# Linear attention's denominators through DRAM, and key-value products of 65 columns

## The chip, the cores and the metric

The kernel runs on one core of one Trainium2 chip. The metric is the device time of one execution in microseconds (us). Times of the kernel before: 1421.81 us, the median of 3 runs (1420.85 to 1428.24).

## What is computed

Three layers follow each other: a linear attention, a feed-forward layer with an ELU, and a mixture of four experts. The change lies in the first.

```python
def phi(x):                                    # 4 batches, 8 heads, 576 tokens, 64 wide; w_phi 64 x 128
    proj = einsum('bhsd,df->bhsf', x, w_phi)
    proj = proj - max(abs(proj), axis=-1)
    return concatenate([exp(proj), exp(-proj)])
q_p, k_p = phi(q), phi(k)
kv  = einsum('bhsf,bhsd->bhfd', k_p, v)
z   = sum(k_p, axis=2)
num = einsum('bhsf,bhfd->bhsd', q_p, kv)
den = einsum('bhsf,bhf->bhs', q_p, z) + 1e-06
x   = num / den                                # 2304 tokens x 512
h   = x @ w_in;  x = where(h > 0, h, exp(min(h, 0)) - 1) @ w_out
x   = sum over 4 experts of p_e * (relu(x @ w1[e]) @ w2[e])
```

## The kernel before

The attention goes over 16 pairs of heads (4 batches, 4 pairs each); `pair(i)` is a Python generator that emits the instructions of one pair in 11 pieces, with a `yield` between pieces. The pieces: project keys and queries with `wbd` (L199 and L221 for pairs 0 to 6 in plain fp32, L201 to L203 as three products of fp32r halves from pair 7 on), subtract the row's largest absolute value (`guard`, L209 and L210 on DVE), take both exponentials on ACT, form the key-value products (`kv`, L242 and L243, 20 matmul instructions a pair with 128x128 weights from `kp` or `kpm` and 128 moving columns from `vt`), transpose the queries' features (L249, L287), and multiply them with the key-value products (`num`, L321, in two halves of 288 tokens).

The tile `vt` holds, for each block of keys, 64 columns of values and 64 columns of ones (L165 fills the tile with 1.0 once, `load` writes the values over one half). So the rows of a `num` result are 64 numerators and 64 equal copies of the denominator. `num` copies the denominators out of PSUM on ACT (L325), `divide` takes the reciprocal of 128x288 on DVE (L330) and multiplies the numerators, still in PSUM, by it (L333). `put_x` stores the result `xf` in DRAM (L301, for a later pass) and splits it into `xh` and `xl` (L307 on ACT, L308 on POOL), which the second stage reads.

The second stage (`Elu`, L530 to L532 up, L559 to L561 down) goes over 9 tiles of 256 tokens, twice (two halves of the hidden width). Tile t of the first half needs all pairs of its batches: 4 pairs before tile 0, 8 before tile 2, 12 before tile 4, 16 before tile 6. Between its instructions `slot()` emits further pieces of the attention (1.4 to a slot) and of the weight conversions. Where a tile's pairs are not yet emitted, L758 emits pieces until they are. `convert64` turns a block of weights into two fp32r halves: a load on SP (L104) into one of three buffers, then ACT, DVE (L115 to L118), POOL, ACT and POOL in turn; 64 such loads belong to the first half. The third stage (`Up`, `Down`) is untouched by the change.

All DMAs are issued on the one SP queue, in order: an issue that waits holds all behind it. A scheduler puts the emitted instructions of each engine into one fixed order when the program is built. The pair's tiles `kq`, `xf` and `rc` have one buffer each, the PSUM pool `bank` has seven.

Of the kernel before, what the change touches and what calls it, by code (L numbers as in the profile page):

```python
# [8 lines left out]
F32 = mybir.dt.float32  # L9
F32R = mybir.dt.float32r  # L10
U32 = mybir.dt.uint32
I64 = mybir.dt.int64
ACTF = mybir.ActivationFunctionType
ALU = mybir.AluOpType
# [3 lines left out]
B, H, S, D, FEAT = 4, 8, 576, 64, 128  # L18
NT, DM, DFF, E, F2 = 2304, 512, 2048, 4, 1024
P = 128  # L20
KD = DM // P
NP = H // 2
# [32 lines left out]
CVP = 16  # L55
CVW = 256
CVOFF = 0
MINF = 2.0 ** -15
MAXF = 122879.9921875

# [2 lines left out]
def attn_elu_moe_kernel(ctx: ExitStack, tc: tile.TileContext, kq_in, vv, w_phi, w_in, w_out, probs, w1, w2, out):  # L63
# [13 lines left out]
    x1fin = [dram.tile([P, KD, TS], F32, name=f"x1fin{t}") for t in range(NTS)]  # L77
    yscr = [dram.tile([P, DM], F32, name=f"yscr{r}") for r in range(NT // P)]
    xvd = [[dram.tile([P, 2, 2, TC], F32, name=f"xvd{g}_{k}") for k in range(7)] for g in range(NG)]
    x1scr = [dram.tile([P, KD, TS], F32, name=f"x1scr{t}") for t in range(NTS)]  # L80
    ring = pool("ring", RING)
    p2 = ExitStack()
# [55 lines left out]
    def load(i):  # L138
        b, p = divmod(i, NP)
        kq = ld.tile([P, 2 * S], F32, tag="kq", name="kq")  # L140
        SP.dma_start(kq[:, :640], kq_in[b, p, :, :640])
        if i == 0:
            SP.dma_start(wbd, w_phi)
        SP.dma_start(kq[:, 640:], kq_in[b, p, :, 640:])
        v = vt[i % 2]
        SP.dma_start(v[:, 0:4, 0:D], vv[b, p, :, 0:4, :])
        SP.dma_start(v[:, 4:8, D:P], vv[b, p, :, 4:8, :])
        SP.dma_start(v[0:D, 8, 0:D], vv[b, p, 0:D, 8, :])
        SP.dma_start(v[0:D, 9, D:P], vv[b, p, D:P, 8, :])
        return kq, v  # L150

    def bank(shape=(P, 512)):
        return psum[0].tile(list(shape), F32, tag="bank", name="bank")
# [7 lines left out]

    make_identity(nc, ident)
    for i in range(2):
        t = a1.tile([P, 10, P], F32, name=f"vt{i}")
        G.memset(t, 1.0)  # L165
        vt.append(t)
    kpm = a1.tile([P, 2, 2, P], F32, name="kpm")
# [8 lines left out]
    def pair(i):  # L176
# [58 lines left out]
        yield  # L235
        guard(qd[1], proj(qh, 1), 4)
        yield
        pk = bank((P, 4, P))

        def kv(h, c):  # L240
            for t in range(4):
# [30 lines left out]
                G.tensor_tensor(out=el[:, h, :, c0:c0 + n], in0=ef[:, h], in1=f32(eh[:, h, :, c0:c0 + n]), op=ALU.subtract)  # L272

        if wide:
            kvw = a1.tile([P, 4, P], F32, tag=("kvh", "kvl")[i % 2], name="kvw")
        else:
            kvh = a1.tile([P, 4, P], F32R, tag="kvh", name="kvh")
            kvl = a1.tile([P, 4, P], F32R, tag="kvl", name="kvl")
        ef0 = qexp(tpose(0), 0, 256)
        kv(0, 0)  # L280
        kv(0, 1)
# [26 lines left out]
                G.tensor_tensor(out=xl[:, p, c:c + n], in0=xf[:, o:o + n], in1=f32(xh[:, p, c:c + n]), op=ALU.subtract)  # L308
                o += n

        rc = a1.tile([P, 2, HS], F32, tag="rc", name="rc")

        def num(s):
            sl = slice(s * HS, (s + 1) * HS)
            pn = [bank() for _ in range(2)]
            terms = ((kvw, ew),) if wide else ((kvh, eh), (kvh, el), (kvl, eh))
            last = 2 * len(terms) - 1
            for h in range(2):
                for k in range(last + 1):
                    c, (w, m) = k // len(terms), terms[k % len(terms)]  # L320
                    PE.matmul(pn[h][:, :HS], w[:, 2 * h + c], m[:, h, c, sl], start=(k == 0), stop=(k == last))  # L321
            for h in range(2):
                r = slice(h * D, h * D + D)
                o = slice(D - h * D, P - h * D)
                A.activation(rc[r, s], pn[h][o, :HS], ACTF.Copy, bias=1e-6)  # L325
            return pn

        def divide(s, pn):
            sl = slice(s * HS, (s + 1) * HS)
            V.reciprocal(out=rc[:, s], in_=rc[:, s])  # L330
            for h in range(2):
                r = slice(h * D, h * D + D)
                V.tensor_tensor(out=xf[r, sl], in0=pn[h][r, :HS], in1=rc[r, s], op=ALU.mult)  # L333

        pn0 = num(0)
        yield
        divide(0, pn0)
        pn1 = num(1)
        yield
        divide(1, pn1)  # L340
        put_x()

    done = [0]
# [545 lines left out]
```

## Time and profile before

| | |
|---|---|
| median of 3 runs | 1421.81 us |
| the profiled execution | 1429.35 us, its span 1427.6 us |
| PE busy | 1385.5 us, 97% |
| PE weight loads busy | 1292.6 us, 91% |
| DVE, ACT, POOL busy | 687.9, 618.2, 440.8 us |
| mean granted TensorE clock | 0.991 of full speed |
| DMA | 160.22 MB, 112 GB/s |

The trace shows two matmuls, each with its weight load, for one plain fp32 matmul instruction of the program (L199, L221, L242, L243, and L321 of pairs 0 to 6), and one for a transpose or an fp32r matmul; so the 20 key-value instructions of a pair stand there as 40.

Busy time of PE is a union of matmul durations that overlap each other, so a busy PE can still issue slowly; what counts is the spacing from one matmul's start to the next. The attention and the first half of the second stage lie in the first 450 us, the third stage in the last 770.

### The profile page before, as it was taken

The numbers are of one execution on the slowest core, as the hardware profiler recorded it, in microseconds if no ns is written. First come the engines' busy times: TensorE is split into PE (matmuls) and PEld (weight loads), VectorE is DVE, ScalarE is ACT, GpSimd is POOL, SyncE is SP. The second block draws the span as 40 slices with busy tenths as digits, with TensorE's granted clock in tenths as the row PEclk, the third lists the DMA queues.
The fourth block names the chain that finished last, engine by engine and source line by source line (L and its number), as shares of the span: only waits on it lengthen the run. The fifth ranks groups of instructions, "written<-read, shape, count | busy, mean of one in ns | idle before, by whom it ended". The sixth has DMA issues, their size and how long they took to land.

```text
span 1427.6 us, 22324 instructions
## 1 busy us (share of the span) xinstructions
PE 1385.5 (97%) x8688; PEld 1292.6 (91%) x8688; DVE 687.9 (48%) x1150; ACT 618.2 (43%) x1348; POOL 440.8 (31%) x499
## 2 busy tenths in 40 slices
PE   7899999999999999999999999999999999999998
PEld 6788999999999999999998989898888989899897
DVE  7987756565477635334434323234433325323332
ACT  6766866666466534344333443122321214321121
POOL 4556754444377713024102340002320005300000
PEclk9999999999999999999999999999999999999999
DMA  5324322120333345313333233434145351433421
GB/s 156 125 87 132 111 62 60 56 70 32 97 98 126 97 159 198 112 46 104 111 133 147 93 107 137 155 111 148 47 146 177 101 200 54 141 111 133 165 79 67
DMA packets 93625, 160.22 MB, mean 112 GB/s; under 512 B 28496, under 2 KB 39888, under 8 KB 93520
## 3 DMA queue, kind: packets, MB, share of 16 engines
q1 hardware_dynamic: 93520, 158.80, 33.6%
q8 instruction: 68, 1.11, 0.3%
q14 instruction: 37, 0.30, 0.1%
HBM read 109.22 MB, written 49.55 MB: 111 GB/s over the span
## 4 chain that ended last, share of the span: by engine, by line
PE 75%; DMA 5%; DVE 4%; ACT 2%; POOL 2%; issue 2%; SPq 0%; DVEq 0%; ACTq 0%; POOLq 0%
PE bank L706 8%; PE bank L707 8%; PE bank L708 8%; PE bank L647 7%; PE bank L649 7%; PE bank L648 7%; PE bank L560 3%; PE bank L559 3%; PE bank L561 3%; PE bank L530 3%; PE bank L532 3%; PE bank L531 3%; PE bank L242 2%; DMA wst<-in_w 2%; PE bank L321 2%
## 5 line engine op out<-in xcount | busy, mean ns | idle before, releaser
L706 PE MATMUL bank<-w,h 128*128 128x512 f32 x576 | 224.6, 392 | 4.7 <-ACT h L658 4.7
L648 PE MATMUL bank<-xv,w 128*128 128x384 f32 x672 | 226.1, 336 | 0.0
L707 PE MATMUL bank<-w,h 128*128 128x512 f32 x576 | 225.6, 392 | 0.0
L647 PE MATMUL bank<-xv,w 128*128 128x384 f32 x672 | 223.8, 339 | 1.0 <-DVE xs L580 0.8
L649 PE MATMUL bank<-xv,w 128*128 128x384 f32 x672 | 223.0, 337 | 0.0
L708 PE MATMUL bank<-w,h 128*128 128x512 f32 x576 | 198.3, 391 | 0.7 <-DVE h L659 0.7
L467 POOL TENSOR_TENSOR w<-wst,w 128x256 fp32r<-128x256 f32 x80 | 62.1, 795 | 349.6 <-ACT w L466 345.4
L560 PE MATMUL bank<-gl,w 128*128 128x256 f32 x576 | 161.1, 284 | 1.8 <-DVE gl L543 1.8
L559 PE MATMUL bank<-gh,w 128*128 128x256 f32 x576 | 155.4, 286 | 5.2 <-ACT gh L542 4.1
L561 PE MATMUL bank<-gh,w 128*128 128x256 f32 x576 | 160.2, 283 | 0.0
L647 PEld LDWEIGHTS bank<-xv,w 128*128 128x128 f32 x672 | 126.2, 188 | 9.0 <-DVE xs L580 1.0
L658 ACT ACTIVATE h<-bank 128x384 fp32r<-128x384 f32 x144 | 66.8, 490 | 152.7 <-PE bank L649 91.6
L659 DVE SCALAR_TENSOR_TENSOR h<-bank,h 128x384 fp32r<-128x384 f32 x144 | 77.3, 553 | 113.5 <-ACT h L658 113.5
L706 PEld LDWEIGHTS bank<-w,h 128*128 128x128 f32 x576 | 108.5, 188 | 25.7 <-ACT h L658 5.9
L648 PEld LDWEIGHTS bank<-xv,w 128*128 128x128 f32 x672 | 126.5, 188 | 4.4
L707 PEld LDWEIGHTS bank<-w,h 128*128 128x128 f32 x576 | 108.6, 189 | 20.6
L649 PEld LDWEIGHTS bank<-xv,w 128*128 128x128 f32 x672 | 125.9, 188 | 0.0
L708 PEld LDWEIGHTS bank<-w,h 128*128 128x128 f32 x576 | 107.3, 188 | 20.1 <-DVE h L659 1.6
L559 PEld LDWEIGHTS bank<-gh,w 128*128 128x128 f32 x576 | 106.1, 191 | 7.3 <-ACT gh L542 5.7
L560 PEld LDWEIGHTS bank<-gl,w 128*128 128x128 f32 x576 | 110.1, 191 | 2.5 <-DVE gl L543 2.4
L561 PEld LDWEIGHTS bank<-gh,w 128*128 128x128 f32 x576 | 110.1, 191 | 0.2 <-POOL w L126 0.2
L653 ACT ACTIVATE cmab<-bank 128x384 f32<-128x384 f32 x48 | 23.6, 492 | 178.5 <-PE bank L649 178.5
(119 smaller groups left out, 2987.3 us busy)
## 6 DMA issues: line engine op xcount, KB each, us to landing
xv<-xvd SPq DMA_DIRECT2D x42, 768.0 KB, 4.4
wst<-in_w SPq DMA_DIRECT2D x64, 256.0 KB, 2.8
xvd<-xv SPq DMA_DIRECT2D x21, 768.0 KB, 4.5
yscr<-y SPq DMA_DIRECT2D x54, 256.0 KB, 2.2
y<-yscr SPq DMA_DIRECT2D x54, 256.0 KB, 2.9
w<-in_w_in SPq DMA_DIRECT2D x32, 256.0 KB, 2.8
w<-in_w_out SPq DMA_DIRECT2D x32, 256.0 KB, 2.7
kq<-in_kq SPq DMA_DIRECT2D x16, 320.0 KB, 3.1
```

The lines of the kernel that those rows point to most:

```text
L467: on[WL[v % len(WL)]].tensor_tensor(out=lo, in0=x, in1=f32(hi), op=ALU.subtract)
L559: PE.matmul(o, w[:, 0, c], self.gh[:, j], start=start, stop=False)
L560: PE.matmul(o, w[:, 0, c], self.gl[:, j], start=False, stop=False)
L561: PE.matmul(o, w[:, 1, c], self.gh[:, j], start=False, stop=stop)
L647: PE.matmul(o, hi[:, c], x[:, 0, kc], start=not more and kc == 0, stop=False, skip_group_check=more)
L648: PE.matmul(o, hi[:, c], x[:, 1, kc], start=False, stop=False, skip_group_check=more)
L649: PE.matmul(o, lo[:, c], x[:, 0, kc], start=False, stop=kc == 1, skip_group_check=more)
L658: A.activation(h[:, 0], c, ACTF.Relu)
L659: V.scalar_tensor_tensor(out=h[:, 1], in0=c, scalar=0.0, in1=f32(h[:, 0]), op0=ALU.max, op1=ALU.subtract)
L706: PE.matmul(self.acc, h[:, 0, c], w[:, 0], start=f == 0, stop=False)
L707: PE.matmul(self.acc, h[:, 0, c], w[:, 1], start=False, stop=False)
L708: PE.matmul(self.acc, h[:, 1, c], w[:, 0], start=False, stop=f == 2 * NQ - 1)
```

## The change

The ones shrink to one column. `vt`, the key-value products, their copies `kvw`, `kvh`, `kvl` and the `num` results get 65 columns (rows) where they had 128: 64 numerators and one denominator. The numerators leave PSUM together with the denominator (the new L325, into `nd[0]` and `nd[1]`, one tile a head for both halves of the tokens). The denominator row of each head (1x576) is written to DRAM (`dscr`), read back as 128x9 (`dn`), gets its 1e-6 and its reciprocal there, is written to DRAM again (`rscr`), and is read back as two rows broadcast over 64 partitions (`rb`). Then one multiplication of 64x576 a head gives `xf`. The pair has 15 pieces instead of 11. The new tiles `nd`, `dn` and `rb` have one buffer each. The lines of the changed kernel lie 2 higher up to the old L321, and 6 higher from the old L343 on.

```diff
--- before.py
+++ after.py
@@ -55,6 +55,7 @@
 CVP = 16
 CVW = 256
 CVOFF = 0
+M1 = D + 1
 MINF = 2.0 ** -15
 MAXF = 122879.9921875
 
@@ -77,6 +78,7 @@
     x1fin = [dram.tile([P, KD, TS], F32, name=f"x1fin{t}") for t in range(NTS)]
     yscr = [dram.tile([P, DM], F32, name=f"yscr{r}") for r in range(NT // P)]
     xvd = [[dram.tile([P, 2, 2, TC], F32, name=f"xvd{g}_{k}") for k in range(7)] for g in range(NG)]
+    dscr, rscr = ([dram.tile([2, S], F32, name=f"{n}{i}") for i in range(B * NP)] for n in ("den", "rec"))
     x1scr = [dram.tile([P, KD, TS], F32, name=f"x1scr{t}") for t in range(NTS)]
     ring = pool("ring", RING)
     p2 = ExitStack()
@@ -144,9 +146,9 @@
         SP.dma_start(kq[:, 640:], kq_in[b, p, :, 640:])
         v = vt[i % 2]
         SP.dma_start(v[:, 0:4, 0:D], vv[b, p, :, 0:4, :])
-        SP.dma_start(v[:, 4:8, D:P], vv[b, p, :, 4:8, :])
+        SP.dma_start(v[:, 4:8, 0:D], vv[b, p, :, 4:8, :])
         SP.dma_start(v[0:D, 8, 0:D], vv[b, p, 0:D, 8, :])
-        SP.dma_start(v[0:D, 9, D:P], vv[b, p, D:P, 8, :])
+        SP.dma_start(v[0:D, 9, 0:D], vv[b, p, D:P, 8, :])
         return kq, v
 
     def bank(shape=(P, 512)):
@@ -161,7 +163,7 @@
 
     make_identity(nc, ident)
     for i in range(2):
-        t = a1.tile([P, 10, P], F32, name=f"vt{i}")
+        t = a1.tile([P, 10, M1], F32, name=f"vt{i}")
         G.memset(t, 1.0)
         vt.append(t)
     kpm = a1.tile([P, 2, 2, P], F32, name="kpm")
@@ -235,7 +237,7 @@
         yield
         guard(qd[1], proj(qh, 1), 4)
         yield
-        pk = bank((P, 4, P))
+        pk = bank()[:, :4 * M1].rearrange("p (n m) -> p n m", m=M1)
 
         def kv(h, c):
             for t in range(4):
@@ -272,10 +274,10 @@
                 G.tensor_tensor(out=el[:, h, :, c0:c0 + n], in0=ef[:, h], in1=f32(eh[:, h, :, c0:c0 + n]), op=ALU.subtract)
 
         if wide:
-            kvw = a1.tile([P, 4, P], F32, tag=("kvh", "kvl")[i % 2], name="kvw")
+            kvw = a1.tile([P, 4, M1], F32, tag=("kvh", "kvl")[i % 2], name="kvw")
         else:
-            kvh = a1.tile([P, 4, P], F32R, tag="kvh", name="kvh")
-            kvl = a1.tile([P, 4, P], F32R, tag="kvl", name="kvl")
+            kvh = a1.tile([P, 4, M1], F32R, tag="kvh", name="kvh")
+            kvl = a1.tile([P, 4, M1], F32R, tag="kvl", name="kvl")
         ef0 = qexp(tpose(0), 0, 256)
         kv(0, 0)
         kv(0, 1)
@@ -308,7 +310,7 @@
                 G.tensor_tensor(out=xl[:, p, c:c + n], in0=xf[:, o:o + n], in1=f32(xh[:, p, c:c + n]), op=ALU.subtract)
                 o += n
 
-        rc = a1.tile([P, 2, HS], F32, tag="rc", name="rc")
+        nd = [a1.tile([M1, S], F32, tag=f"nd{h}", name=f"nd{h}") for h in range(2)]
 
         def num(s):
             sl = slice(s * HS, (s + 1) * HS)
@@ -318,26 +320,30 @@
             for h in range(2):
                 for k in range(last + 1):
                     c, (w, m) = k // len(terms), terms[k % len(terms)]
-                    PE.matmul(pn[h][:, :HS], w[:, 2 * h + c], m[:, h, c, sl], start=(k == 0), stop=(k == last))
+                    PE.matmul(pn[h][:M1, :HS], w[:, 2 * h + c], m[:, h, c, sl], start=(k == 0), stop=(k == last))
             for h in range(2):
-                r = slice(h * D, h * D + D)
-                o = slice(D - h * D, P - h * D)
-                A.activation(rc[r, s], pn[h][o, :HS], ACTF.Copy, bias=1e-6)
-            return pn
-
-        def divide(s, pn):
-            sl = slice(s * HS, (s + 1) * HS)
-            V.reciprocal(out=rc[:, s], in_=rc[:, s])
-            for h in range(2):
-                r = slice(h * D, h * D + D)
-                V.tensor_tensor(out=xf[r, sl], in0=pn[h][r, :HS], in1=rc[r, s], op=ALU.mult)
-
-        pn0 = num(0)
-        yield
-        divide(0, pn0)
-        pn1 = num(1)
-        yield
-        divide(1, pn1)
+                A.activation(nd[h][:, sl], pn[h][:M1, :HS], ACTF.Copy)
+
+        num(0)
+        yield
+        num(1)
+        yield
+        for h in range(2):
+            SP.dma_start(dscr[i][h:h + 1, :], nd[h][D:M1, :])
+        yield
+        dn = a1.tile([P, S // D], F32, tag="dn", name="dn")
+        SP.dma_start(dn, dscr[i].rearrange("h (a b) -> (h a) b", b=S // D))
+        yield
+        V.tensor_scalar(out=dn, in0=dn, scalar1=1e-6, scalar2=None, op0=ALU.add)
+        V.reciprocal(out=dn, in_=dn)
+        SP.dma_start(rscr[i].rearrange("h (a b) -> (h a) b", b=S // D), dn)
+        yield
+        rb = a1.tile([D, 2, S], F32, tag="rb", name="rb")
+        for h in range(2):
+            SP.dma_start(rb[:, h], rscr[i][h:h + 1, :].broadcast_to([D, S]))
+        yield
+        for h in range(2):
+            V.tensor_tensor(out=xf[h * D:h * D + D], in0=nd[h][:D], in1=rb[:, h], op=ALU.mult)
         put_x()
 
     done = [0]
```

The order of instructions moves at many places, for the scheduler places everything anew. Three places follow.

First, PE at the start of the second stage. `kp_853`, `kp_854` before and `kp_945`, `kp_946` now are pair 4's keys; L530 and L536 are the first matmul of tile 0. Before:

```order
L321 MATMUL bank<-ew,kvw 128x288 x4
L199 MATMUL bank<-wbd,kq 128x256 x2
L249 MATMUL bank<-ident,qd_856 128x128 x4
...
L242 MATMUL bank<-vt_172,kp_853 128x128 x2
L242 MATMUL bank<-vt_172,kp_854 128x128 x2
L243 MATMUL bank<-vt_172,kpm 128x128
L530 MATMUL bank<-xh,w 128x256
L531 MATMUL bank<-xl,w 128x256
L532 MATMUL bank<-xh,w 128x256
```

Now:

```order
L244 MATMUL bank<-vt_204,kp_945 128x65 x2
L244 MATMUL bank<-vt_204,kp_946 128x65 x2
L245 MATMUL bank<-vt_204,kpm 128x65
L223 MATMUL bank<-wbd,kq 128x256
L251 MATMUL bank<-ident,qd_949 128x128 x4
L289 MATMUL bank<-ident,md 128x128 x2
L201 MATMUL bank<-wbd,kq 128x256 x4
L323 MATMUL bank<-ew,kvw 65x288 x2
L201 MATMUL bank<-wbd,kq 128x256 x2
L323 MATMUL bank<-ew,kvw 65x288 x6
L536 MATMUL bank<-xh,w 128x256
```

Before, 15 of pair 4's 20 key-value matmuls stand ahead of tile 0; now all 20 do, and with them 1 and 6 projections of pair 5's (L223 and L201), 6 transposes and all 8 `num` matmuls of pair 4.

Second, the SP queue at the end of pair 0, now. `den` and `rec` are the DRAM tiles `dscr` and `rscr`; `w` are loads of weights for conversion, `vt_206` the values of pair 3:

```order
L332 DMA den_124<-nd_410 1x576
L143 DMA kq<-in_kq 128x640
L146 DMA kq<-in_kq 128x512
L335 DMA dn<-den_124 128x9
L106 DMA w_555<-in_w_in 128x256
...
L339 DMA rec_140<-dn 128x9
L106 DMA w_606<-in_w_in 128x256
L151 DMA vt_206<-in_vv 64x64
L343 DMA rb<-rec_140 64x576 x2
L106 DMA w_649<-in_w_in 128x256
L303 DMA xscr_0_60<-xf 128x576
```

Before, a pair had only the last of these; now six more issues stand in the queue, with one to three weight loads between those of one pair. Up to the last `rb` of pair 3 the queue now holds 24 weight loads; before, up to the `xscr` of pair 3, it held 18.

Third, PE between the last pair's `num` and tile 6, the first tile that needs that pair (the rows left out go on in the same threes). Now:

```order
L323 MATMUL bank<-el,kvh 65x288
L323 MATMUL bank<-eh,kvl 65x288
L565 MATMUL bank<-gh,w 128x256
L566 MATMUL bank<-gl,w 128x256
...
L536 MATMUL bank<-xh,w 128x256
L537 MATMUL bank<-xl,w 128x256
L538 MATMUL bank<-xh,w 128x256
...
L565 MATMUL bank<-gh,w 128x256
L566 MATMUL bank<-gl,w 128x256
```

Of the matmuls between that last `num` and tile 6's first, 12 are L565 to L567, then 24 are L536 to L538 of tile 5, then 24 are L565 to L567. At tile 2 stand, between the same two, 19 projections, 24 Elu matmuls, 10 transposes, 20 key-value and 14 `num` matmuls and one L223; at tile 4, 48 Elu, 24 `num` and else the same.

## Rows read from the trace of the kernel before

**Rows 1.** The page, part 1: busy time of each engine, its share and instructions.

```profile
PE 1385.5 (97%) x8688; PEld 1292.6 (91%) x8688; DVE 687.9 (48%) x1150; ACT 618.2 (43%) x1348; POOL 440.8 (31%) x499
```

**Rows 2.** The table by stage: busy time of each engine, granted clock, DMA share.

```profile
0.00:82.00 82.00, 67.61 (x392) 59.44 (x393) 70.50 (x138) 55.71 (x137) 42.49 (x65) 0.96 0.45 137
82.00:150.00 68.00, 62.75 (x417) 56.91 (x417) 56.63 (x113) 45.77 (x116) 46.59 (x63) 0.92 0.34 109
150.00:345.00 195.00, 194.24 (x1611) 192.84 (x1610) 123.83 (x178) 133.24 (x298) 98.26 (x105) 1.00 0.21 66
345.00:375.00 30.00, 26.48 (x208) 26.10 (x207) 14.72 (x21) 14.38 (x32) 9.92 (x12) 0.94 0.13 38
```

**Rows 3.** Waits of PE from 0 to 82 us: total, times, longest.

```profile
PE bank L249 <- DVE qd L210: 7.0, 3, 4.8
PE bank L249 <- DVE prs L97: 2.9, 1, 2.9
```

**Rows 4.** Waits of PE from 82 to 150 us.

```profile
PE bank L559 <- ACT gh L542: 1.8, 1, 1.8
PE bank L530 <- ACT w L124: 1.5, 1, 1.5
PE bank L559 <- ACT w L124: 1.0, 1, 1.0
PE bank L321 <- DVE qd L210: 0.7, 1, 0.7
```

**Rows 5.** Waits of PE from 345 to 375 us.

```profile
PE bank L249 <- DVE qd L210: 2.7, 1, 2.7
```

**Rows 6.** Timeline of DVE ahead of that wait.

```profile
340.87 3.99 DVE L330 RECIPROCAL rc<-rc 128x288 f32<-128x288 f32 x2
```

**Rows 7.** The chain that ended last: start, time, matmuls back to back.

```profile
148.59 0.97 PE bank L321 x4
160.91 0.89 PE bank L242 x8
173.37 1.58 PE bank L321 x12
```

**Rows 8.** Timeline of PE: two Elu matmuls of 256 columns that follow each other.

```profile
339.40 0.28 PE L560 MATMUL bank<-gl,w 128*128 128x256 f32 x1
339.52 0.28 PE L561 MATMUL bank<-gh,w 128*128 128x256 f32 x1
```

**Rows 9.** Lines 242 and 249: weight loads, ns least, median and most.

```profile
L242 PEld LDWEIGHTS bank<-vt,kp x512: 187/192/338, 13.8 to 355.5; 128*128 128x128 f32 x171
L249 PEld LDWEIGHTS bank<-ident,qd x128: 137/140/230, 13.4 to 353.3; 128*128 128x128 f32 x128
```

**Rows 10.** Costliest groups of DVE from 0 to 150 us: mean ns.

```profile
L330 DVE RECIPROCAL rc<-rc 128x288 f32<-128x288 f32 x12 | 23.3, 1944 | 0.6 <-ACT rc L325 0.6
L210 DVE TENSOR_TENSOR kp<-bank,mx 128x512 f32<-128x512 f32 x16 | 10.8, 679 | 0.0
L333 DVE TENSOR_TENSOR xf<-bank,rc 64x288 f32<-64x288 f32 x24 | 10.7, 447 | 0.3
L99 DVE RECIPROCAL prr<-prs 128x18 f32<-128x18 f32 x1 | 0.3, 252 | 0.0
```

**Rows 11.** Lines 325 and 307 of ACT: denominators out of PSUM, and output split.

```profile
L325 ACT ACTIVATE rc<-bank x64: 402/406/411, 23.1 to 364.7; 64x288 f32<-64x288 f32 x64
L307 ACT ACTIVATE xh<-xf 128x256 fp32r<-128x256 f32 (+3 forms) x18 | 5.9, 361 | 9.3 <-DVE xf L333 9.2
```

**Rows 12.** DMA issues from 0 to 150 us: KB each, median us to landing.

```profile
xscr<-xf SPq DMA_DIRECT2D x6, 288.0 KB, 2.3
vt<-in_vv SPq DMA_DIRECT2D x18, 16.0 KB, 2.5
```

**Rows 13.** Waits of the SP queue from 0 to 150 us.

```profile
SPq L104 <- DVE top L117: 69.9, 30, 9.3
```

**Rows 14.** Timeline of PE: the first matmul of the second stage.

```profile
81.51 0.36 PE L530 MATMUL bank<-xh,w 128*128 128x256 f32 x1
```

## The prediction

> **What bounds the kernel now.** I read the page's engine list first: PE is busy 97% of the span and no other engine half of it [rows 1]. That is an average over stages, so the table by stage comes next [rows 2]. The change touches pairs that run in the first 375 us. From 150 to 345 us PE is busy 194 of 195 us at full clock: there only PE's own work counts, and a faster DVE or ACT buys nothing. From 0 to 82 us and from 82 to 150 us it is otherwise. PE is busy 67.6 of 82 and 62.8 of 68 us, and the granted clock is 0.96 and 0.92, while DVE is busy 70.5 of 82 us. A granted clock of 0.92 means that 16% of the stretch, 10.9 us, ran at 1.2 instead of 2.4 GHz, which loses 5.4 us of work.
>
> The waits of PE tell what ends its idle time. Up to 82 us it is DVE's `qd` (7.0 us) and a small DVE reduction (2.9 us) [rows 3]. From 82 to 150 us it is ACT's `gh`, converted weights and `qd` again: 1.8 + 1.5 + 1.0 + 0.7 = 5.0 us [rows 4], so with the clock 10.4 us are lost. From 345 to 375 us it is `qd` once more, 2.7 us [rows 5], and a clock of 0.94, 1.8 us. So the gain that can be had is in these stages, some 25 us in all, and in PE's work itself.
>
> **Key-value products of 65 columns.** The trace has 640 of them, two for each instruction of the program, and 8 take 0.89 us back to back, 111 ns each [rows 7]. `num` in plain fp32 takes 0.97 us for 4, so 243 ns for 288 columns, 0.84 ns a column. By moving columns alone 128 cost 108 ns, which is nearly the 111 seen, and 65 would cost 55, say 58 with the same 3 ns on top: 53 ns saved in each, 34 us. But each of these matmuls loads its own 128x128 weights, and the change leaves those as they are. The weight load of the products takes 192 ns, that of the transposes, of the same shape, 140 [rows 9]. The 52 ns between are 128 columns at 2.4 GHz (53 ns); at the slow clock, where the longest of each stand, 338 and 230 ns, they are 108, 128 columns at 1.2 GHz. I read this as one pass over the columns for a transpose and two for a plain fp32 weight, so 107 ns in which the next load can't begin. Then the spacing stays at 107 to 111 ns, whatever moves. I take 0 us, with 24 us as the other end: of the 34 us, the part of the some 450 products that lie after 82 us, 450 x 53 ns. The end below nothing I leave at 0, since nothing in them grows.
>
> The rule of the Trainium skill (TensorE: Matmul & The Clock Gate, section LDWEIGHTS) is that a weight load takes its columns divided by 1.2 in ns, whatever the rows, so 107 ns for 128. By that rule the products would gain at most 4 ns each, 2.6 us in all; the trace agrees with it in the difference of the two weight loads, and no run here shows a product narrower than its weights.
>
> `num` keeps its 288 moving columns: 243 ns in fp32, 1.58 us for 12, 132 ns, as fp32r [rows 7]. Its weight loads fall from 128 to 65 columns, which the moving columns hide already: 0 us.
>
> **DVE.** A pair loses two reciprocals of 1.94 us and four multiplications of 0.45 us, together 5.7 us [rows 10]. It gets two multiplications of 64x576, which no row shows; between one of 64x288 (0.45) and two (0.9) I take the 0.7 of the nearest, 128x512 from PSUM. The 128x9 addition and reciprocal cost at most 0.25 us each (the 128x18 reciprocal). So 3.8 us of DVE go per pair. Where PE is full that is worth nothing. On ACT four copies of 65 rows replace four of 64 (0.41 us each [rows 11]), the copy of the key-value products about halves; POOL fills half the ones once. These have slack under PE: 0 us; were the cover gone, it would be a gain.
>
> **The new chain.** In the place of one reciprocal a pair waits for four DMAs in a row. From the first copy into `nd`: four copies 4 x 0.41 = 1.6 us; the write to DRAM 2.3 (as `xscr`, 288 KB); the read 2.5 (as the 16 KB loads of `vt`) [rows 12]; addition and reciprocal 0.5; the second write 2.3; the broadcast read 2.5; one multiplication 0.7. Sum 12.4 us. The pieces of 36 bytes have no row; the 16 KB loads in pieces of 256 bytes are the nearest. Two things come on top. All issues are on SP, and SP stood 69.9 of the first 150 us at weight loads that waited for a free buffer, 2.3 us a time, at most 9.3 [rows 13]; the order shows one to three such loads between the issues of one pair. For an issue that meets this half of the time and half through a wait I take 0.5 us, 2 us for four. And ACT and DVE are in order: three visits of some 0.7 us (the instruction ahead) are 2.1. That makes 16.5 us. Its ends: 14.5, with half of these additions, and 21.6, with a whole wait of 2.3 us for each issue.
>
> `nd` has one buffer a head. So the next pair's first copy waits for this pair's multiplication, and in the first stage the chain is the **period of a pair**. The first copy starts at 23.1 us [rows 11]. After four periods, a second multiplication (0.7) and `xh` (0.4 [rows 11]), tile 0 can begin: 23.1 + 4 x 16.5 + 1.1 = 90.2 us, where it was 81.5 [rows 14], 8.7 us later. But the order puts more work of PE ahead of it, the plain fp32 instructions counting twice: 10 products and 6 transposes at 0.111, 14 projections (0.84 ns x 256 columns, 0.22 each) and 16 `num` at 0.243, so 1.8 + 3.0 + 3.9 = 8.7 us. **Start: 0 us**, with ends of -8 (14.5 us) and +20 (21.6).
>
> **82 to 150 us.** Of the 10.4 us lost there, DVE's 5 to 6 pairs' share of 3.8 us and the six weight conversions more that are ahead should return the greater part. I take **-7 us**; ends 0 and -10.4.
>
> **Where a tile waits for its last pair.** From the pair's last `num` the chain has one copy 0.4, two writes and two reads 9.6, DVE 0.5, both multiplications 1.4 and `xh` 0.4, which is 12.3, with hand-overs some 13 us. Elu matmuls follow each other by 0.12 us [rows 8]. At tile 6 stand 60 of them, 7.1 us: 5.9 us open. At tile 2: 24 of them and 19 projections at 0.12, 10 transposes and 20 products (twice) at 0.111, 14 `num` at 0.132 and one L223 (twice 0.22), 12.9 us: 0.1 open. At tile 4, with 24 Elu and 10 `num` more, 17.1 us: covered. **+6.0 us**; ends +2 and +12 (the chain at 17). Against it the loss at 345 us, where `qd` stood behind two reciprocals, 4.0 us [rows 6], goes: 2.7 + 1.8 = **-4.5 us**, other end 0.
>
> Elsewhere the chain hides: in the full stretch a pair's share of PE is half a tile of Elu (96 matmuls at 0.12) and of its own 24 at 0.12, 24 at 0.132, 50 at 0.111 and two of 0.22, 24 us in all, against 16.5.
>
> **Sum:** 0 + 0 - 7 + 6.0 - 4.5 = -5.5 us. The profiled execution took 1429.35 us, so 1423.9. It was the slowest shown, 7.5 us over the median; I carry the difference to the median, 1421.8 - 5.5 = **1416 us**. About 0.5% (7 us) can be told from no change by a measurement here, so the forecast is no change that can be told, 1.6 us from the bound.
>
> **Rivals.**
> A. The products cost their 65 moving columns after all. For it: 111 ns is nearly 108, and the rows of 288 columns lie on the same line. Against it: the weight loads. Time 1416 - 24 = 1392 us. Chance 0.13.
> B. DVE was the bound of the first 150 us, and the chain is short. For it: 70.5 of 82 us busy, and the longest wait of PE in the first stage, 4.8 us, is for DVE. With a period of 14.5 us the start gives -8 instead of 0, and the second stretch all its 10.4: 1416 - 8 - 3.4 = 1405 us. Against it: `nd` has one buffer. Chance 0.12.
> C. Slower: the DMAs of the chain stand behind weight loads on SP. For it: SP stood there 47% of the first 150 us; the order puts 24 loads, not 18, ahead of pair 3's last read. A period of 20 us instead of 16.5 costs 4 x 3.5 = 14 us: 1430 us. It decides from a period of 19.7 us, where 4 x 3.2 = 12.6 us more pass the upper bound (1429). Against it: a lighter DVE frees the conversion buffers sooner. Chance 0.15.
> D. DVE and ACT, in order, stand for the chain in the full stretch as well, Elu's `g` and `gh` come late, and PE waits, say 1.5 us for each of 11 pairs: 1432 us. Against it: one step of 24 matmuls, 2.9 us, lies between `gh` and its use. Chance 0.08.
>
> **How the numbers follow.** The forecast has the rest, 0.52, with a range of its own from 1408 to 1425; as the bound (1414.7) lies just under it, 0.20 of the 0.52 counts as faster and 0.32 as the same. Faster is then 0.20 + 0.13 + 0.12 = 0.45, the same 0.32, slower 0.15 + 0.08 = 0.23. The range reaches from 1395 us (B and a part of A; the rest of A out) to 1435 us (C with a period of 21, the worst out).
>
> **What would show it.** Products 105 to 111 ns apart (at 58 A holds). From one pair's first `nd` copy to the next one's 15 to 18 us in the first 90 us; first matmul of tile 0 at 86 to 96 us. Granted clock over 0.95 from there to 150 us. A wait of PE for `xh` or `xl` of some 6 us ahead of tile 6 and about none ahead of tiles 2 and 4. SP's waits at weight loads of no more than before. I am wrong if tile 0 starts before 84 or after 98 us, or if the products are near 60 ns.

## The result and the profile after

The changed kernel takes 1434.88 us (median of 6 runs, 1430.48 to 1443.22) against 1422.58 us for the kernel before beside it: 1.0082 times as long, with a 95% interval of 1.0059 to 1.0106. That is slower by 0.8%, 12 us, where the forecast was 1416 us. The range (1395 to 1435) just holds it, but the direction is wrong. The profiled execution has a span of 1431.3 us.

The page's engine list, which answers to [rows 1]: DVE lost 56 us of work, and the kernel got no faster by it.

```profile
PE 1389.4 (97%) x8688; PEld 1291.7 (90%) x8688; DVE 631.4 (44%) x1118; ACT 608.7 (43%) x1348; POOL 442.5 (31%) x499
```

The table by stage after (start and end, length, then busy time of PE, PEld, DVE, ACT and POOL, granted clock, DMA share, GB/s), which answers to [rows 2], with one stretch more:

```profile
0.00:82.00 82.00, 70.84 (x356) 58.71 (x357) 58.96 (x136) 52.69 (x137) 44.40 (x67) 0.88 0.51 144
82.00:150.00 68.00, 65.89 (x480) 59.34 (x478) 51.47 (x116) 49.39 (x128) 50.79 (x69) 1.00 0.49 142
150.00:345.00 195.00, 189.26 (x1553) 186.23 (x1552) 89.32 (x147) 122.98 (x286) 94.76 (x97) 0.99 0.24 71
345.00:375.00 30.00, 30.00 (x253) 29.89 (x251) 7.62 (x15) 13.82 (x32) 7.86 (x9) 1.00 0.14 43
375.00:460.00 85.00, 73.91 (x574) 71.80 (x573) 54.23 (x110) 48.08 (x111) 56.16 (x69) 0.96 0.36 113
```

A busy PE can still run at half clock, so I use one measure for all kernels below: **lost time**, the spacing from each group of matmuls to the next, less what the group takes back to back at full clock (0.111 us a key-value matmul or transpose, 0.119 an Elu matmul, 0.217 a plain fp32 projection, 0.243 or 0.132 a `num` matmul). It holds idle time and half clock together. The names of the runs are those of the experiments below.

| lost us in | 0 to 82 | 82 to 150 | 150 to 345 | 345 to 375 | 375 to 460 | sum |
|---|---|---|---|---|---|---|
| before | 13.9 | 11.3 | 0.2 | 5.4 | 4.4 | 35.2 |
| the change | 18.3 | 4.2 | 7.2 | 2.6 | 14.1 | 46.4 |
| e1, before in 15 pieces | 14.6 | 6.6 | 21.4 | -0.2 | 6.1 | 48.5 |
| e2, before without reciprocals | 8.4 | 1.0 | -0.3 | 0.0 | 3.1 | 12.2 |
| f6, e1 at a pace of 1.9 | 13.7 | 4.7 | 0.2 | 1.3 | 4.3 | 24.2 |
| g4, f6 without reciprocals | 6.9 | 0.1 | -0.9 | -0.1 | 4.8 | 10.8 |
| f3, the change at 1.9 | 18.8 | 10.2 | -0.8 | 0.0 | 4.9 | 33.1 |
| h3, f3 with four edits | 12.2 | 2.7 | 3.3 | -0.2 | 3.2 | 21.2 |

The change loses 11.2 us more than the kernel before up to 460 us, which is nearly the whole 12. The two profiled executions as wholes differ by 3.7 us only (spans of 1431.3 and 1427.6): from the second half of the second stage on, which the change does not touch, the one of the kernel before took 7 us longer, so the table is read by stages, and the medians decide on the times. Three places show how the time is lost.

**Ahead of tile 6.** Timeline of SP, then of DVE (start, time, line, operation; in brackets the idle time ahead and its releaser), then of ACT, then the two waits of PE there:

```profile
365.25 1.03 SPq L332 DMA_DIRECT2D den<-nd  x2
367.23 0.34 SPq L335 DMA_DIRECT2D dn<-den  x1
371.01 0.34 SPq L339 DMA_DIRECT2D rec<-dn  x1
373.12 1.09 SPq L343 DMA_DIRECT2D rb<-rec  x2
```

```profile
370.56 0.17 DVE L337 TENSOR_SCALAR dn<-dn 128x9 f32<-128x9 f32 x1 [6.15 <-DMA dn<-den]
376.34 0.75 DVE L346 TENSOR_TENSOR xf<-nd,rb 64x576 f32<-64x576 f32 x1 [4.47 <-DMA rb<-rec]
377.02 0.68 DVE L549 TENSOR_TENSOR gl<-g,gh 128x512 fp32r<-128x512 f32 x1
377.73 0.75 DVE L346 TENSOR_TENSOR xf<-nd,rb 64x576 f32<-64x576 f32 x1
```

```profile
387.54 1.06 ACT L512 ACTIVATE x2h<-xst 128x1024 fp32r<-128x1024 f32 x1 [2.15 <-DMA xst<-xscr]
388.50 0.61 ACT L548 ACTIVATE gh<-g 128x512 fp32r<-128x512 f32 x1
```

```profile
377.75 0.39 PE L566 MATMUL bank<-gl,w 128*128 128x256 f32 x1 [2.65 <-DVE gl L549]
389.17 0.80 PE L565 MATMUL bank<-gh,w 128*128 128x256 f32 x2 [3.48 <-ACT gh L548]
```

The chain takes 11.1 us from the write of the denominators to the first multiplication and 13.2 to the end of the second. The first 18 matmuls of tile 6 read the other pairs' results and run at 372.56 to 374.70, so the tile does not wait as a whole. The first wait of PE, 2.65 us, is for `gl` of the tile before, which stands on DVE behind the multiplication. The second, 3.48 us, has another place: `gh` stands on ACT behind a copy that waits 2.15 us for `xst`, the read of the attention's result for the second half, and SP issues these reads at 378.93 and 383.26, behind the write of `xf`, which waits for the multiplications, and a write of the tile before.

**Ahead of tile 2**, in the stretch where PE was full before, timeline of DVE, then of PE:

```profile
190.01 2.51 DVE L346 TENSOR_TENSOR xf<-nd,rb 64x576 f32<-64x576 f32 x2 [2.97 <-DMA rb<-rec]
192.54 1.29 DVE L211 TENSOR_REDUCE mx<-bank 128x4 f32<-128x512 f32 x2
194.35 0.42 DVE L296 TENSOR_TENSOR kvl<-bank,kvh 128x260 fp32r<-128x260 f32 x1
```

```profile
194.82 0.51 PE L323 MATMUL bank<-eh,kvl 128*65 128x288 f32 x1 [2.52 <-DVE kvl L296]
```

**In the first stage**, again DVE (with the first multiplications of the other three pairs) and then PE, whose matmuls after the wait run at half clock (a granted clock of 0.50 from 61.7 to 70 us; 8 products take 1.60 us to the next group's start instead of 0.89); the last line is tile 0's first matmul, 81.51 before [rows 14]:

```profile
38.31 0.75 DVE L346 TENSOR_TENSOR xf<-nd,rb 64x576 f32<-64x576 f32 x1 [1.22 <-DMA rb<-rec]
...
58.03 0.75 DVE L346 TENSOR_TENSOR xf<-nd,rb 64x576 f32<-64x576 f32 x1 [2.33 <-DMA rb<-rec]
59.94 0.69 DVE L211 TENSOR_REDUCE mx<-bank 128x4 f32<-128x512 f32 x1
60.87 0.68 DVE L212 TENSOR_TENSOR qd<-bank,mx 128x512 f32<-128x512 f32 x1
...
78.43 0.74 DVE L346 TENSOR_TENSOR xf<-nd,rb 64x576 f32<-64x576 f32 x1
...
95.24 1.53 DVE L346 TENSOR_TENSOR xf<-nd,rb 64x576 f32<-64x576 f32 x2 [0.98 <-DMA rb<-rec]
```

```profile
61.70 1.09 PE L251 MATMUL bank<-ident,qd 128*128 128x128 f32 x4 [2.57 <-DVE qd L212]
62.58 1.81 PE L244 MATMUL bank<-vt,kp 128*128 128x65 f32 x8
...
94.22 0.50 PE L536 MATMUL bank<-xh,w 128*128 128x256 f32 x1
```

The products themselves did not change. Timeline of PE: eight of them with 65 columns take 0.89 us from their start to the next group's (166.66 to 167.55), 111 ns each, as with 128 columns [rows 7].

```profile
166.43 0.39 PE L245 MATMUL bank<-vt,kpm 128*128 128x65 f32 x2
166.66 1.06 PE L244 MATMUL bank<-vt,kp 128*128 128x65 f32 x8
167.55 0.39 PE L245 MATMUL bank<-vt,kpm 128*128 128x65 f32 x2
```

What a load of weights costs by its columns is seen at `num`, whose weights went from 128 to 65 columns. Its weight loads from 150 to 345 us, before and now (ns least, median and most):

```profile
L321 PEld LDWEIGHTS bank<-eh,kvh x64: 187/188/192, 173.1 to 341.2; 128*128 128x128 f32 x64
L323 PEld LDWEIGHTS bank<-eh,kvh x62: 134/136/232, 173.7 to 344.7; 128*65 128x65 f32 x62
```

63 columns less take 52 ns less, 0.83 ns a column; by that 128 columns take some 106 ns, an estimate from these two rows. The 111 ns of the products lie just above it.

### The profile page after: what moved, and what is told of

It reads as the page before. It is cut to its first block, busy times and chain, and to the rows that moved or that the text cites. A ratio compares the mean times of both kernels' runs of the same rounds, so it can differ in the third digit from the quotient of the medians.

```text
span 1431.3 us, 22497 instructions
## 1 busy us (share of the span) xinstructions
PE 1389.4 (97%) x8688; PEld 1291.7 (90%) x8688; DVE 631.4 (44%) x1118; ACT 608.7 (43%) x1348; POOL 442.5 (31%) x499
## 4 chain that ended last, share of the span: by engine, by line
PE 77%; DMA 7%; DVE 5%; POOL 3%; ACT 2%; issue 2%; SPq 1%; DVEq 0%; POOLq 0%; ACTq 0%
PE bank L712 9%; PE bank L713 8%; PE bank L714 8%; PE bank L653 8%; PE bank L655 8%; PE bank L654 8%; PE bank L566 3%; PE bank L536 3%; PE bank L567 3%; PE bank L565 3%; PE bank L537 3%; PE bank L538 3%; PE bank L244 2%; PE bank L323 2%; DMA rb<-rec 2%
## 5 line engine op out<-in xcount | busy, mean ns | idle before, releaser
L565 PE MATMUL bank<-gh,w 128*128 128x256 f32 x576 | 157.2, 287 | 5.5 <-ACT gh L548 5.5
L567 PE MATMUL bank<-gh,w 128*128 128x256 f32 x576 | 161.3, 284 | 0.0
L712 PEld LDWEIGHTS bank<-w,h 128*128 128x128 f32 x576 | 108.2, 188 | 23.9 <-ACT h L664 4.1
L565 PEld LDWEIGHTS bank<-gh,w 128*128 128x128 f32 x576 | 107.4, 193 | 6.5 <-ACT gh L548 6.3
L567 PEld LDWEIGHTS bank<-gh,w 128*128 128x128 f32 x576 | 111.0, 193 | 0.1
```

The lines of the kernel that those rows point to most:

```text
L565: PE.matmul(o, w[:, 0, c], self.gh[:, j], start=start, stop=False)
L567: PE.matmul(o, w[:, 1, c], self.gh[:, j], start=False, stop=stop)
L712: PE.matmul(self.acc, h[:, 0, c], w[:, 0], start=f == 0, stop=False)
```

## The experiments

Every edit also gives the scheduler another program, and so another order of the instructions on each engine; differences of 2 or 3 us are not explained here, and e3 below shows that an edit which changes no duration can be worth 9 us. All medians are of several runs beside the kernel before (1422.6 to 1423.9 us).

**First batch: what each part costs.** e1: the kernel before with the change's number of pieces.

```diff
         pn1 = num(1)
         yield
+        yield
+        yield
+        yield
+        yield
         divide(1, pn1)
```

> The kernel before with four empty pieces ahead of the last one, so 15 pieces a pair as in the change, and nothing else. Theory of the waits (the change loses because DVE, ACT and SP, each in order, stand for the four DMAs in a row): within 5 us of the kernel before. Rival, the pacing (15 pieces need 60 slots for four pairs where 45 are given, so attention is emitted in bursts and the order gets worse): most of the 12 us, 1430 us or more.

Measured 1435.76 us, ratio 1.0084 (1.0061 to 1.0108): without a DMA or a column changed, the pieces alone cost as much as the change. The waits of PE from 150 to 375 us (engine, buffer, line, releaser: total, times, longest) show a wait that the kernel before did not have:

```profile
PE bank L249 <- ACT gh L546: 9.5, 2, 5.2
PE bank L563 <- ACT gh L546: 2.4, 1, 2.4
```

e2: the reciprocals left out (`V.reciprocal` at L330 deleted).

> The kernel before without its reciprocals (left out: the numerators are multiplied by the denominators). What the 1.94 us of DVE, 32 times, are worth by themselves. If DVE bounds the first 150 us, as I took it, 8 to 14 us faster than before (1408 to 1415 us); if the attention is bound by something else there, within 5 us of before.

Measured 1402.92 us, ratio 0.9856 (0.9835 to 0.9876): 20 us, of which 16 lie in the first 150 us by the table. The relief of DVE is real and larger than I had taken it, and larger than the 8 to 14 us expected.

e3 (the first two lines; the wider `vt` and the copies of 65 columns are left out here): 128 moving columns as before, of which 65 are copied; e4 (the other lines): all DMAs of the chain issued, but the reads take constant tiles, filled once at the start.

```diff
-        pk = bank()[:, :4 * M1].rearrange("p (n m) -> p n m", m=M1)
+        pk = bank((P, 4, P))
...
-        SP.dma_start(dn, dscr[i].rearrange("h (a b) -> (h a) b", b=S // D))
+        SP.dma_start(dn, dcon.rearrange("h (a b) -> (h a) b", b=S // D))
...
-            SP.dma_start(rb[:, h], rscr[i][h:h + 1, :].broadcast_to([D, S]))
+            SP.dma_start(rb[:, h], rcon[h:h + 1, :].broadcast_to([D, S]))
```

> The change, but with 64 columns of ones again in the key-value products (128 moving columns); only 65 of them are copied and used, and the denominators go by DMA as in the change. If a product costs its weight load (111 ns in both traces), the same time as the change within 4 us and products 111 ns apart; if columns count, 20 us slower than the change.

> The change with all its DMAs, but the two reads take constant DRAM tiles written once at the start, so no leg waits for the one before (left out: the true denominators). Theory of the waits: the 12 us go and DVE's relief shows, 1408 to 1420 us, and no wait of DVE for a read of denominators. Rival, the load (six more issues a pair on SP and small packets on the DMA engines): as the change, 1430 to 1438 us.

Measured 1426.09 us (ratio 1.0012, 0.9998 to 1.0027) and 1424.03 us (1.0005, 0.9995 to 1.0016), 9 and 11 us less than the change. As a product takes 111 ns at either width, e3 pointed to the order; e4 pointed to the waits but gave nothing of the relief back.

**Second batch: the pace.** `slot()` gives 1.4 pieces, which over two tiles of 16 slots each makes 45: enough for four pairs of 11 pieces, not for four of 15. What is left is emitted in one go ahead of tiles 2, 4 and 6. f3 and f6 set the pace for 15 pieces (1.4 x 15 / 11 = 1.9), on the change and on e1; f1 takes the four additional pieces out of the change instead.

```diff
-RATE = 1.4
+RATE = 1.9
```

> The change with the pace of the pairs raised from 1.4 to 1.9 pieces a slot, so that the slots of two tiles give 61 pieces, enough for four pairs of 15, where they gave 45; nothing is left out. Theory P (the pieces left over are done in one go ahead of tiles 2 and 4, and that bunching is what the four additional pieces cost): the 12 us that the additional pieces cost in the kernel before come back, 1435 - 12 = 1423 us. Theory W (what costs is DVE and ACT standing for the chain's DMAs): the pieces of a chain come closer to each other in time, so the waits stay or grow, 1433 to 1440 us.

> The kernel before with four empty pieces a pair, as run already at 1435.8 us, and with the pace raised to 1.9; nothing is left out. Theory P: 1424 us, as the kernel before. Rival (the cost of the empty pieces is the first stage, where each piece carries two steps of the weight stream, and the pace does not act there): stays at 1433 to 1437 us.

> The change with its whole chain, from the write of the denominators to the last multiplication, in one piece, so that a pair has 11 pieces as before; nothing is left out. Theory P: 1435 - 12 = 1423 us. Theory W: the chain's waits now have nothing of other pieces planned between them in the order of the program, and DVE and PE wait for them: 1438 us or more, with DVE's waits for the read of the denominators and of the reciprocals longer than the 37 us in all that the change shows for the latter.

Measured: f3 1424.15 us (ratio 1.0010, 0.9990 to 1.0031), f6 1416.78 us (0.9963, 0.9951 to 0.9974), f1 1427.35 us (1.0045, 1.0024 to 1.0066). On both kernels theory P is the nearer one: the pace takes back 11 us of the change and 19 us of e1, 7 more than the empty pieces had cost. In the table the losses after 150 us are gone, 23.9 us in the change and 4.1 in f3; ahead of 150 us f3 loses 6.5 us more than the change. f1, 4 us above theory P and far below theory W, fits too: 6.6 us are lost there after 150 us, but 38.9 before, since the chain in one piece makes the first stage worse. But DVE stands at the multiplication for `rb` in f3 nearly as long as in the change (waits of DVE up to 460 us, the change and then f3):

```profile
DVE xf L346 <- DMA rb<-rec: 37.2, 16, 4.9
DVE xf L346 <- DMA rb<-rec: 34.1, 16, 5.3
```

So the pace did not shorten the waits; they no longer have something behind them that PE needs at once. And the pace is not alone in it: e4 kept 15 pieces at 1.4, but its reads do not wait for the chain, and PE is as full from 150 to 345 us as in f3 (f3, then e4):

```profile
150.00:345.00 195.00, 195.00 (x1627) 193.65 (x1626) 92.00 (x153) 125.10 (x289) 95.54 (x99) 1.00 0.25 73
150.00:345.00 195.00, 193.82 (x1609) 191.19 (x1608) 90.53 (x143) 129.24 (x298) 97.45 (x103) 1.00 0.24 74
```

In the change the loss after 150 us is gone without the bunched pieces (f3), and without the waits (e4). Bunched pieces can cost without the chain too, as e1 shows with its reciprocals; why they cost nothing in e4 is not shown. What the pace gives depends on the kernel: 19 us on e1, 11 on the change, but 4 on e3 (g5 below) and 2 on e4 (f8 below). The kernel before with 11 pieces at 1.9 was not run, so how much of f6's gain is the faster pace by itself is open.

The timeline of PE in f3 shows no place like the two above after 150 us; what f3 still has is the first stage (table by stage, then DVE, then PE):

```profile
0.00:82.00 82.00, 65.38 (x355) 53.43 (x355) 58.99 (x135) 53.41 (x138) 43.04 (x68) 0.93 0.49 143
82.00:150.00 68.00, 64.09 (x410) 57.96 (x411) 53.90 (x114) 47.13 (x123) 50.21 (x67) 0.89 0.47 138
```

```profile
60.36 0.91 DVE L346 TENSOR_TENSOR xf<-nd,rb 64x576 f32<-64x576 f32 x1 [1.72 <-DMA rb<-rec]
61.64 0.75 DVE L346 TENSOR_TENSOR xf<-nd,rb 64x576 f32<-64x576 f32 x1
62.43 0.69 DVE L211 TENSOR_REDUCE mx<-bank 128x4 f32<-128x512 f32 x1
63.36 0.69 DVE L212 TENSOR_TENSOR qd<-bank,mx 128x512 f32<-128x512 f32 x1
```

```profile
64.19 0.63 PE L251 MATMUL bank<-ident,qd 128*128 128x128 f32 x4 [2.53 <-DVE qd L212]
81.97 1.09 PE L251 MATMUL bank<-ident,qd 128*128 128x128 f32 x4 [4.24 <-DVE qd L212]
```

f4 tried to keep the gain of e2 without the chain: logarithm and exponential on ACT in the place of the reciprocal.

```diff
-            V.reciprocal(out=rc[:, s], in_=rc[:, s])
+            A.activation(rc[:, s], rc[:, s], ACTF.Ln)
+            A.activation(rc[:, s], rc[:, s], ACTF.Exp, scale=-1.0)
```

> The kernel before with each 128x288 reciprocal on DVE (1.94 us) replaced by two operations on ACT, the logarithm and the exponential of its negative (some 0.45 us each, by ACT's copies of that width); nothing is left out. The run without any reciprocal took 1403 us. Theory DVE (the reciprocals' time on DVE is what costs): 1403 us plus what ACT's 29 us more cost, of which most lies under PE: 1405 to 1410 us. Rival (ACT is as late as DVE at these places, or has to change its function tables at each logarithm): 1420 us or more, with waits of PE for ACT in the place of those for DVE.

Measured 1458.75 us (1.0259, 1.0244 to 1.0274): the rival. The groups of ACT up to 460 us show a change of tables at every logarithm, and as many again at the exponentials that come next (the largest groups):

```profile
L330 ACT ACT_TABLE_LOAD x32 | 41.1, 1283 | 0.6
L331 ACT ACT_TABLE_LOAD x18 | 23.1, 1283 | 0.3
L214 ACT ACT_TABLE_LOAD x9 | 11.5, 1283 | 0.2
L330 ACT ACTIVATE rc<-rc 128x288 f32<-128x288 f32 x32 | 14.2, 445 | 0.4
```

The logarithm is 0.45 us as expected; the 59 table loads shown cost 76 us of ACT. That they make the time is read from this trace; no run takes them away alone. The Trainium skill (ScalarE: Activation LUTs, section Table sets: the hidden batching unit) lists one set with both functions, by which one load would do; this program, as it was compiled, did not get by with one.

**Third batch: what is left at equal pieces and pace.** From f3: the multiplication on POOL (g1), two buffers for `nd` (g3), 128 columns (g5); from f6: no reciprocals (g4).

```diff
-            V.tensor_tensor(out=xf[h * D:h * D + D], in0=nd[h][:D], in1=rb[:, h], op=ALU.mult)
+            G.tensor_tensor(out=xf[h * D:h * D + D], in0=nd[h][:D], in1=rb[:, h], op=ALU.mult)
```

> The change at the pace of 1.9, with its last two multiplications on POOL instead of DVE; nothing is left out. At this pace the change took 1424.2 us, and the kernel before with as many pieces 1416.8, 7.4 us less; the trace of the former shows PE waiting 1.6, 2.5 and 4.2 us for `qd` in the first 82 us, each time with DVE standing at the multiplication for the reciprocals' read. Theory W (DVE standing for the read is what is left of the loss): these waits go, and 5 to 8 us with them, 1416 to 1419 us. Rival (the period of a pair, which the single `nd` sets, is what is left, whichever engine multiplies): 1422 us or more.

> The change at the pace of 1.9, with two buffers for each `nd`, so that the next pair's copies need not wait for this pair's multiplication; nothing is left out. Theory W: nothing changes, since DVE still stands for the read ahead of `qd`, 1422 to 1427 us. Rival (the period set by the single `nd`): tile 0 begins some 8 us earlier than its 100.0 us, and the time is 1416 to 1419 us.

> The kernel before with four empty pieces a pair and the pace of 1.9 (1416.8 us), with its 128x288 reciprocals left out, so that the products are not divided. It prices the relief of DVE at the pieces and the pace of the change. If the relief is the same as at 11 pieces (20 us): 1397 us. If the smoother pace has already taken what the reciprocals cost after 150 us (10 us of loss are left, of them 18 in the first 150 us with the half clock): 1403 to 1408 us.

> The change at the pace of 1.9, with 128 moving columns in the key-value products, of which the 65 are copied; nothing else differs, and the products take the same 111 ns in the traces. At the pace of 1.4 the 128 columns made it 8.8 us faster, which I lay to another order of the instructions. If that is an accident of the order at that pace: 1420 to 1427 us, within 4 us of the 1424.2 with 65. If 65 columns themselves cost time: 1415 us, 9 us less.

Measured: g1 1421.67 us (0.9986, 0.9967 to 1.0005), g3 1423.16 (0.9993, 0.9975 to 1.0011), g4 1403.10 (0.9851, 0.9831 to 0.9872), g5 1421.66 (0.9988, 0.9968 to 1.0008). So the 9 us of the 128 columns at the old pace (e3) do not stand at the new one, which speaks for an accident of the order, and a second `nd` alone changes nothing in the time that can be told. g4 prices the relief at this pace: 1416.8 - 1403.1 = 13.7 us (16 by the two ratios, as f6 and g4 were measured beside different runs of the kernel before). The change has this relief and stands at 1424.2, so all that it has in the place of the reciprocals, here called its **chain, costs 21 us**, and by the table 22 of lost time lie in the first 150 us (29.0 in f3, 7.0 in g4). g1 is short of what theory W promised: PE's waits for `qd` go, but the next one takes their place (waits of PE from 0 to 150 us):

```profile
PE bank L223 <- DMA kq<-in_kq: 4.9, 5, 1.5
```

The load of `kq` stands on SP behind a write of the denominators, which waits for `nd`.

**Fourth batch: SP's order.** From g1, one edit more each time: the writes of `den` on ACT's queue (h1), two `nd` (h2), the write of `xscr` on ACT's queue (h3). f8 is e4 at the pace of 1.9.

```diff
-            SP.dma_start(dscr[i][h:h + 1, :], nd[h][D:M1, :])
+            A.dma_start(dscr[i][h:h + 1, :], nd[h][D:M1, :])
...
-            SP.dma_start(xscr[b][p], xf)
+            A.dma_start(xscr[b][p], xf)
```

> The change at the pace of 1.9 with its multiplications on POOL (1421.7 us), and now with the writes of the denominators on ACT's queue instead of SP's; nothing is left out. Its trace had PE waiting 4.9 us in the first 150 us for the next pair's `kq`, whose load stands on SP behind those writes, which wait for `nd`. Theory C (what is left is SP's order): these 5 us go, 1414 to 1418 us. Rival (the period of a pair, set by the single `nd`): the wait moves to ACT, which then stands at its copies, and the time stays at 1420 to 1424 us.

> As the run before it in this list, with two buffers for each `nd`; nothing is left out. By theory C alone no change to that run. If the single `nd` binds once DVE and SP no longer do: 4 to 8 us less than that run, 1408 to 1414 us, with tile 0 beginning at 80 to 85 us.

> As the run before it in this list, and with the write of a pair's result to DRAM on ACT's queue too, so that the next pair's `kq` stands behind nothing of the chain but its two reads and one write; nothing is left out. If SP's order still costs: 2 to 5 us less than that run. If not: within 2 us of it. The bound for all these runs is what the kernel before takes at these pieces and this pace without its reciprocals, 1403 us.

> The change at the pace of 1.9, all of its DMAs issued, but its reads take constant tiles in DRAM, so that the true denominators are left out of the result; the writes and SP's order stay. At the pace of 1.4 this took 11 us off. Theory W (the waits for the read data are the rest of the loss): 1424 - 8 = 1416 us or less. Theory C (SP's order, which stays here): 1420 to 1424 us, with PE waiting for `kq`.

Measured: h1 1421.50 us (0.9986, 0.9964 to 1.0009), h2 1418.95 (0.9962, 0.9939 to 0.9984), h3 1416.96 (0.9954, 0.9935 to 0.9973), f8 1422.23 (0.9986, 0.9967 to 1.0006). No single step can be told from the one before it; h1 misses theory C, and f8 misses theory W. Together the four edits give 7 us: the intervals of f3 and h3 lie apart. h3's waits of PE from 0 to 150 us are neither for `qd` nor, but for 0.5 us, for `kq`:

```profile
PE bank L323 <- ACT kvw L293: 4.9, 3, 2.3
PE bank L223 <- DMA wbd<-in_w_phi: 4.2, 1, 4.2
PE bank L323 <- ACT ew L264: 2.9, 1, 2.9
```

f8 lies where theory C had it, 1420 to 1424, but does not settle whether waits for data or SP's order cost more: its reads are still issued late, and DVE still stands for their landing (waits of DVE from 0 to 150 us):

```profile
DVE dn L342 <- DMA dn<-dcon: 19.6, 13, 3.0
```

h3 and f6 are the versions that beat both kernels, by 0.46% and 0.37% of the kernel before.

## Why the prediction was wrong

By the stages of the sum, predicted and measured in lost time (the change less before):

| term | predicted | measured |
|---|---|---|
| start, 0 to 82 us | 0 | +4.4 |
| 82 to 150 us | -7 | -7.1 |
| 150 to 345 us: tiles 2 and 4 covered, "elsewhere the chain hides" | 0 | +7.0 |
| loss at 345 us | -4.5 | -2.8 |
| tile 6's last pair, 375 to 460 us | +6.0 | +9.7 |

The -7.1 us are in part luck: f3, with the same relief and chain, loses 10.2 us from 82 to 150 us, nearly as much as the kernel before.

- **Products: right.** 0 us; rival A falls. Half the moving columns left the spacing at 111 ns, so these columns do not set it; the loads of the 128x128 weights fit, with the 106 ns estimated above, though no run narrows the products' own weights. The rule of the Trainium skill that the prediction weighed against the rows (TensorE: Matmul & The Clock Gate, section LDWEIGHTS), 107 ns for such a load, agrees with this trace. It agrees by the `num` loads, 52 ns less for 63 columns less. The prediction's evidence, two passes for a plain fp32 weight against one for a transpose, was misread: before the change the fp32r loads of `num` took 188 ns as well.
- **The chain's length: nearly right.** At tile 6 it takes 13.2 us, with the copy ahead and `xh` behind (0.4 us each) 14, for 13 predicted. In the first stage the first `nd` copy starts at 22.8 us and the four pairs' first multiplications at 38.3, 58.0, 78.4 and 95.2, a mean period of 18.1 us for 16.5, inside its ends (14.5 and 21.6, the latter without the 2.1 us of visits), though above the 15 to 18 named as its sign. Tile 0's first matmul came at 94.2 instead of 90.2, as forecast within 86 to 96, but that is in part luck: it reads pair 0 alone and ran before the fourth pair's multiplication, for which the forecast let it wait. And the reason was wrong: I laid the period to the single `nd`; g3 gave it a second buffer, its first multiplications still came 18 us apart, and it gained nothing in time that can be told.
- **"Elsewhere the chain hides", and tiles 2 and 4 covered: this step failed.** I compared the chain's length with the matmuls beside it, and took 0 us from 150 to 345 us; 7.0 us were lost there. What decides is which instructions stand behind the waiting one on DVE, as rival D had it, and when PE needs them. DVE stood 37.2 us in all at the multiplication for `rb` up to 460 us, and where `kvl`, `qd` or `gl` stood behind it PE stood 2.5 to 2.65 us for each of these three at the places shown. Rival D had 0.08; its 1432 us are the nearest to the result. At the pace of 1.9 the step holds after all (f3 loses nothing from 150 to 345 us), so it failed together with the next one.
- **A term was missing: the pace.** I counted the work that the longer list of pieces puts ahead of tile 0, but not that 15 pieces at a rate set for 11 leave a rest of pieces ahead of tiles 2, 4 and 6. e1 shows its price without the chain, 12 us; f3 shows 11 in the change, more than half of the 19 us between forecast and result. In the change as it stands the losses after 150 us come and go with it. It is no fixed price: with reads that do not wait (e4 against f8) it is 2 us.
- **Relief and chain were both too small.** The relief is worth 20 us at 11 pieces (e2) and 13.7 at 15 (g4), where I had 11.5; the chain costs 21 us at the pace of 1.9, where I had 6.0. The sum in measured steps: 1422.6, pieces and their pace -5.8 (f6), relief -13.7 (g4), chain +21.1 (f3), the old pace +10.7, gives 1434.9. These steps lead from one kernel to the other, so their sum comes out by itself and proves nothing; each step is a difference of two runs.
- **Rivals B and C.** B was right that DVE bounds the first 150 us, but wrong on the short period. C falls: SP's waits at weight loads fell from 69.9 us [rows 13] to 26.2 (waits of SP from 0 to 150 us). SP's order shows elsewhere, in g1's waits for `kq`.

```profile
SPq L106 <- DVE top L119: 26.2, 19, 3.6
```

The granted clock multiplies what a wait costs. In f3 two waits that end at 64.2 and 82.0 us are 2.5 and 4.2 us long, and after the second the products run at the lower level for 11 us (a granted clock of 0.50 from 82 to 93 us); the clock of the stretch from 82 to 150 us is 0.89. After the first they run at full speed, while the wait of 2.57 us in the change was followed by 8 us at 0.50.

**Open:** of the chain's 21 us, 7 are found (DVE's place for the multiplication, SP's order and the second `nd`, together, not each). In the remaining 14 the waits for `kvw` and `ew` on ACT are what PE shows, with no experiment on them; g4 too waits 3.0 us for `kvw`, and the wait for `wbd` (4.1 to 4.3 us) stands in the kernel before as well. That the scheduler takes 65 columns for cheaper products, and so orders the program differently, was only inferred from e3 and g5.

## What to carry to other kernels

Where a generator's pieces are given out at a fixed rate, a change that adds pieces changes the rate too: price that with empty pieces first. Whether a long chain of small DMAs is hidden was decided here by what stands behind the waiting instructions, on each in-order engine and on the DMA queue, and not by its length against the work beside it: after 150 us DVE stood 28.1 us for `rb` in the change and 26.3 in f3, and PE lost 23.9 us in the one and 4.1 in the other. The relief of an engine can be worth more than the waits for it: PE waited 10.5 us for `qd` before, and e2 gave 20 us; the granted clock of 0.96 and 0.92 in the first two stretches [rows 2] rose to 0.98 and 1.00 there.

## What the runs showed that was not expected

A DMA in pieces of 36 bytes (`dn`, 4.5 KB) was used 3.3 us after its issue at tile 6 (367.23 to 370.56, with DVE idle and waiting for it), where the 16 KB loads in [rows 12] landed after 2.5 us. A change of ACT's tables took 1.28 us each time. And four empty pieces in a generator, which emit nothing, moved this kernel by 0.8% in one direction, and with a suitable pace by 0.4% in the other.
